# Padding between SBUF pools: six distances between weights and streamed rows in place of one

## The chip, the cores and the metric

One core of one Trainium2 chip. The metric is the device time of the whole program in microseconds (us). The kernel before was timed twice.

## The reference

The input `x` has 8 sequences of 3072 rows and 256 columns, all float32. The reference takes a real FFT along the 3072 rows of each sequence, mixes the 256 channels of the spectrum by two complex weight matrices, shrinks the result, transforms back, and puts every row through a gated feed-forward block of width 1536:

```python
X = np.fft.rfft(x, axis=1)
Yr = Xr @ w_r - Xi @ w_i + b_r
Yi = Xr @ w_i + Xi @ w_r + b_i
Y = soft(Yr) + 1j * soft(Yi)          # sign(v) * max(|v| - 0.01, 0)
y = np.fft.irfft(Y, n=3072, axis=1).reshape(-1, 256)
rms = np.sqrt(np.mean(y * y, axis=-1, keepdims=True) + 1e-06)
yn = y / rms * rms_g
out = (silu(yn @ w_gate) * (yn @ w_val)) @ w_out
```

## The kernel before, in words

**The products.** Most matrix products are made in float32r. A float32 operand is cut into a high part and the rest (two float32r tiles side by side), and a product is three matmuls: high by high, high by rest, rest by high. A matmul has a weight operand (`lhsT`, 128 x 128, loaded by a weight load of its own) and rows that stream beside it (`rhs`, 256 or 512 columns). The weight load of the next matmul runs beside the matmul that is streaming.

**The stages.** The FFT of 3072 is a 24-point part on VectorE (`first`, `dft8`, `dft3`) and twelve units of 128-point products on TensorE. In `unit` (L506) a unit is: forward (L530, bank `pf`, weights `as`, rows `F`, named `tab` in the profile), mixing (L570, L588, L592, bank `pm`, weights `xs` and, for the first unit, `d`; rows `wm`), and back (L633, L650, L655, bank `pb`, weights `G`, named `tab`; rows `ss`). The first sequence goes through `unit_start` (L672), whose mixing is at L710 with weights `xs` from pool `w2` and rows `wm`, and whose forward and back products (L688, L729) are plain float32. `transposes` (L862) turns four blocks of 128 rows at L867 with `ident`.

The feed-forward block runs in 576 steps: 48 tiles of 512 rows by 12 slices of 128 hidden columns. A step is `straight` (L892; six matmuls of 512 columns at L901 for the gate bank `g` and six for the value bank `v`) or `products` (L915; seven products of half the rows, three matmuls of 256 columns each, at L925), then `down` (L960), twelve matmuls of 256 columns into `acc`. The weights of the up products are `wb`, resident, and `tr` (called `tb` or `tr` in the profile), fetched for each step; the rows are `xn`. The weights of the down product are `hs`, the step's own result, and the rows are `wo`, fetched. 456 steps go by `products` and 120 by `straight`.

**What sets the order.** Every operation goes into a plan (`Plan`) with a due time and a cost; `schedule` plays the engines through and writes one fixed order for each engine. Forward, mixing and back products of the next sequence lie between the feed-forward steps of the one before. On TensorE runs of three matmuls of one kind alternate with runs of another. The plan knows nothing of addresses.

**Where tiles lie.** A pool is a stretch of SBUF, the same in each partition, and pools are laid one behind the other in the order in which they are made (L272 and L273): first `cp` (`wm`), `bp` (the sequences), `w1` (`F`, `ss` and others), `w2` (`xn`, `h`), `w4` (`wo`), which hold all streamed rows of the float32r products; then `wp`, which holds one tile of 320 bytes that nothing reads; then `cq` (`wb`), `q4` (`tr`), `q3` (`hs`), `q1` (`G`, `as`, `xs` and three tiles that are no weights), `q2` (empty) and `sp` (`ident`, biases and small things). All tiles of the pools before `sp`, but for the pad, are of a multiple of 512 bytes in each partition, and a weight operand is a slice of 512 bytes that begins at a multiple of 512 in its tile; rows begin at a multiple of 1024 in theirs. So each weight operand of the pools behind `wp` begins 320 bytes (modulo 512) from the rows beside it.

```python
wp.tile([P, 320], mybir.dt.uint8, name="shift")
```

The table `POOLS` (L326) says which tag lives in which pool with how many buffers.

Of the kernel before, what the change touches and what calls it, by code (L numbers as in the profile page):

```python
# [260 lines left out]
def fourier_glu_kernel(ctx: ExitStack, tc: tile.TileContext, x, w_r, w_i, b_r, b_i, wg, wv, wo, rg, tabs, units, tws, out):  # L261
# [3 lines left out]
    P = 128  # L265
# [3 lines left out]
    def sbuf(name, bufs):  # L269
        return ctx.enter_context(tc.tile_pool(name=name, bufs=bufs))  # L270

    cp, bp, w1, w2, w4 = sbuf("cp", 1), sbuf("bp", 2), sbuf("w1", 1), sbuf("w2", 2), sbuf("w4", 4)  # L272
    wp, cq, q4, q3, q1, q2, sp = sbuf("wp", 1), sbuf("cq", 1), sbuf("q4", 4), sbuf("q3", 3), sbuf("q1", 1), sbuf("q2", 2), sbuf("sp", 1)  # L273
    pu = ctx.enter_context(tc.tile_pool(name="pu", bufs=2, space=bass.MemoryType.PSUM))
    pv = ctx.enter_context(tc.tile_pool(name="pv", bufs=3, space=bass.MemoryType.PSUM))
    pa = ctx.enter_context(tc.tile_pool(name="pa", bufs=1, space=bass.MemoryType.PSUM))
# [3 lines left out]
    V, A, PE, G = nc.vector, nc.scalar, nc.tensor, nc.gpsimd  # L280

    wp.tile([P, 320], mybir.dt.uint8, name="shift")
    wm = cp.tile([P, 2, 2, 3, D], F32R, name="wm")
    wb = cq.tile([P, NF, 3, 2, P], F32R, name="wb")
    dw = [[dp.tile([P, 2, n], F32, name=f"d{c}{i}") for i in range(NF)] for c, n in (("t", 512), ("o", D), ("b", 512))]
# [33 lines left out]
    def add(n, f, r, w):  # L321
# [4 lines left out]
    POOLS = {  # L326
        "seq": (bp, 2), "F": (w1, 1), "t4": (w1, 1), "o": (w1, 1), "m": (w1, 1), "a": (w1, 1), "k": (w1, 1), "z": (w1, 1),
        "ss": (w1, 1), "xf": (w1, 1), "xn": (w2, 2), "h": (w2, 2), "wo": (w4, 4),
        "tr": (q4, 4), "hs": (q3, 3), "G": (q1, 1), "as": (q1, 1), "xs": (q1, 1), "t3": (q1, 1), "st": (q1, 1), "pq": (q1, 1),
        "gb": (pu, 2), "vb": (pv, 3), "acc": (pa, 1), "f": (pf, 1),  # L330
    }

# [949 lines left out]
```

## Time and profile before

| | us |
|---|---|
| median of two timed runs | 2841.64 (2840.09 to 2843.18) |
| the profiled execution's own time | 2839.71 |
| its span, from the first to the last instruction | 2838.0 |
| TensorE matmuls, busy (98% of the span) | 2787.4 |
| TensorE weight loads, busy (95%) | 2702.2 |
| VectorE, busy (81%) | 2297.4 |
| ScalarE, busy (67%) | 1906.8 |
| GpSimd, busy (3%) | 90.4 |

PE stands for TensorE's matmuls, PEld for its weight loads, DVE for VectorE, ACT for ScalarE, POOL for GpSimd. A line such as `L925 PE MATMUL v<-xn,tr` is the instructions of line 925 that write bank `v` from `xn` and `tr`. The time that a matmul is shown to take reaches past the start of the next one; the time from one start to the next is its pace. The timeline merges instructions of the same line and tiles that follow one another: its columns are the start of the first, the time to the end of the last, and, at the end of the line, how many they are. [...]

### The profile page before, as it was taken

The page shows a single profiled execution, that of the slowest core. Times are in us where ns is not written, and L with a number is a line of the kernel's source. Part 1 is how long each engine was busy: PE and PEld are TensorE (multiplying, and loading weights), DVE is VectorE, ACT ScalarE, POOL GpSimd, SP SyncE. Part 2 cuts the span into 40 slices and gives each one's busy share as a digit, 9 for nine tenths or more (in the row PEclk, how much of TensorE's full clock was granted, in tenths as well). Part 3 has the DMA queues.
Part 4 walks back from the last instruction along what each step waited for, and adds up shares of the span by engine and source line. Part 5 has one row for each costly group of instructions (what it writes and reads, how often), then busy time and mean ns, then how long its engine had stood idle before and what let it go on. Part 6 is the DMA issues. An engine that isn't in the chain of part 4 may idle for free.

```text
span 2838.0 us, 57978 instructions
## 1 busy us (share of the span) xinstructions
PE 2787.4 (98%) x22147; PEld 2702.2 (95%) x22147; DVE 2297.4 (81%) x4211; ACT 1906.8 (67%) x4518; POOL 90.4 (3%) x176
## 2 busy tenths in 40 slices
PE   7879999999999999999999999999999999999999
PEld 7768999999999999999999999999999999999999
DVE  9898779977897788977889778987779877866665
ACT  3464676777766777676776667767677677766665
POOL 0000000000000000000000000000000000000000
PEclk9989999999999999999999999999999999999999
DMA  6366665666656667566675666656665677646665
GB/s 213 129 217 201 203 218 174 216 217 216 214 179 214 216 216 231 165 211 212 212 233 172 210 214 220 215 184 210 213 224 190 192 224 220 198 132 223 208 218 171
DMA packets 247033, 577.77 MB, mean 204 GB/s; under 512 B 23393, under 2 KB 80098, under 8 KB 246754
## 3 DMA queue, kind: packets, MB, share of 16 engines
q1 hardware_dynamic: 222562, 485.97, 52.7%
q0 software_dynamic: 24192, 88.09, 10.7%
q8 instruction: 174, 2.85, 0.4%
q14 instruction: 105, 0.86, 0.1%
HBM read 534.65 MB, written 39.32 MB: 202 GB/s over the span
## 4 chain that ended last, share of the span: by engine, by line
PE 96%; DVE 3%; DMA 0%; ACT 0%; issue 0%; SPq 0%; ACTq 0%; DVEq 0%
PE acc L960 28%; PE v L925 22%; PE g L925 17%; PE v L901 6%; PE g L901 6%; PE pf L530 4%; PE pm L592 4%; PE pm L588 2%; PE pb L655 2%; PE pt L867 2%; PE pb L650 1%; PE pm L710 1%; PE pm L570 1%; PE pb L729 1%; PE pf L688 0%; PE pb L633 0%
## 5 line engine op out<-in xcount | busy, mean ns | idle before, releaser
L960 PE MATMUL acc<-wo,hs 128*128 128x256 f32 x6912 | 986.8, 279 | 11.0 <-ACT sq L751 9.0
L960 PEld LDWEIGHTS acc<-wo,hs 128*128 128x128 f32 x6912 | 888.9, 189 | 19.8 <-ACT sq L751 9.1
L925 PE MATMUL v<-xn,tr 128*128 128x256 f32 x4104 | 682.3, 280 | 0.5 <-ACT v L934 0.5
L925 PEld LDWEIGHTS v<-xn,tr 128*128 128x128 f32 x4104 | 567.6, 188 | 2.4 <-ACT v L934 0.7
L952 ACT ACTIVATE hs<-h 128x512 fp32r<-128x512 f32 x576 | 362.4, 629 | 209.9 <-PE acc L960 181.8
L953 DVE TENSOR_TENSOR hs<-h,hs 128x512 fp32r<-128x512 f32 x576 | 395.2, 686 | 83.3 <-ACT hs L952 83.2
L925 PE MATMUL g<-xn,wb 128*128 128x256 f32 x2736 | 457.9, 279 | 0.0
L938 DVE TENSOR_TENSOR y<-v,p 128x512 f32<-128x512 f32 x456 | 314.0, 689 | 174.1 <-PE v L925 165.8
L925 PEld LDWEIGHTS g<-xn,wb 128*128 128x128 f32 x2736 | 378.9, 188 | 0.0
L942 DVE TENSOR_TENSOR h<-h,y 128x512 f32<-128x512 f32 x456 | 313.5, 687 | 66.7 <-ACT h L941 63.6
L941 ACT ACTIVATE h<-v 128x256 f32<-128x256 f32 x456 | 174.0, 382 | 98.1 <-PE v L925 93.0
L925 PE MATMUL g<-xn,tr 128*128 128x256 f32 x1368 | 232.4, 279 | 0.0
L925 PE MATMUL v<-xn,wb 128*128 128x256 f32 x1368 | 232.3, 278 | 0.0
L934 ACT ACTIVATE v<-v 128x256 f32<-128x256 f32 x456 | 169.7, 372 | 92.7 <-PE v L925 90.5
L939 ACT ACTIVATE h<-g 128x256 f32<-128x256 f32 x456 | 174.4, 382 | 68.5 <-PE g L925 62.7
L931 ACT ACTIVATE v<-g 128x256 f32<-128x256 f32 x456 | 169.7, 372 | 73.2 <-PE g L925 69.6
L901 PE MATMUL g<-xn,wb 128*128 128x512 f32 x720 | 190.8, 400 | 1.2 <-DVE wb L810 0.5
L925 PEld LDWEIGHTS g<-xn,tr 128*128 128x128 f32 x1368 | 191.4, 188 | 0.0
L925 PEld LDWEIGHTS v<-xn,wb 128*128 128x128 f32 x1368 | 191.4, 188 | 0.0
L503 POOL DMA_DIRECT2D tab<-in_tabs_dram x168 | 89.6, 533 | 2358.8 <-PE pf L530 1434.3
L901 PEld LDWEIGHTS g<-xn,wb 128*128 128x128 f32 x720 | 129.9, 190 | 26.6 <-DVE wb L810 0.8
L530 PE MATMUL pf<-tab,as 128*128 128x256 f32 x1008 | 138.9, 278 | 0.0
(166 smaller groups left out, 4008.0 us busy)
## 6 DMA issues: line engine op xcount, KB each, us to landing
tr<-dt SPq DMA_DIRECT2D x456, 512.0 KB, 3.9
wo<-do SPq DMA_DIRECT2D x564, 256.0 KB, 3.3
tab<-in_tabs_dram POOLq DMA_DIRECT2D x168, 512.0 KB, 4.7
out_dram<-o SPq DMA_DIRECT2D x32, 512.0 KB, 3.6
seq<-in_x_dram SPq DMA_DIRECT2D x28, 512.0 KB, 5.4
tb<-db SPq DMA_DIRECT2D x27, 512.0 KB, 4.3
seq<-in_x_dram SPq DMA_DIRECT2D x25, 256.0 KB, 5.3
unit<-in_units_dram SPq DMA_DIRECT2D x12, 512.0 KB, 3.6
```

Source lines behind the costliest of these rows:

```text
L530: PE.matmul(ps[:, h, :], lhsT=r()[:, lp, ri, h * P:(h + 1) * P], rhs=f[:, rp, ri, :], start=(k + ri == 0), stop=(k == 2 and ri == 1),)
L901: PE.matmul((g, v)[k].flat(), lhsT=w(k, lp, c), rhs=xn()[:, rp, 2 * c:2 * c + 2, :].rearrange("p a b -> p (a b)"), start=((lp, rp, c) == t ...
L925: PE.matmul(dst(), lhsT=w(lp), rhs=xn()[:, rp, x, :], start=start and k == 0, stop=k == 2, skip_group_check=True)
L931: op("A", act(256), lambda _: A.activation(left(), p1(), AF.Copy), [one.tok], two.first)
L934: op("A", act(256), lambda _: A.activation(right(), left(), AF.Copy), [], [two.tok])
L938: op("V", dve(512), lambda _: V.tensor_tensor(y(), two(), p5().unsqueeze(1).to_broadcast([P, 2, 256]), ALU.add), [two.tok, p5.tok], y.first)
L939: op("A", act(256), lambda _: A.activation(s()[:, :256], p1(), AF.Silu), [one.tok], s.first)
L941: op("A", act(256), lambda _: A.activation(s()[:, 256:], right(), AF.Silu), [two.tok], [s.part("b")])
L942: op("V", dve(512), lambda _: V.tensor_tensor(s(), s(), y().rearrange("p a b -> p (a b)"), ALU.mult), [y.tok, s.part("b")], [s.tok])
L952: op("A", act(512), lambda _: A.activation(h()[:, 0], s(), AF.Copy), [s.tok], h.first)
L953: add(512, lambda f: f(h()[:, 1], s(), f32(h()[:, 0]), ALU.subtract), [s.tok], [h.tok])
L960: PE.matmul(o()[:, c, :], lhsT=h()[:, lp, c * P:(c + 1) * P], rhs=wo_()[:, rp, :], start=(i == 0 and k == 0 and c % 2 == 0), stop=(i == NF ...
```

## The change

The one pad of 320 bytes ahead of all weight pools is replaced by pads of 64 or 128 bytes ahead of single pools, so that the offsets add up. `q1` is split: `as`, `xs` and `G` get pools of their own (`qa`, `qx`, `qg`), and what was left of it stays in `q1`. The empty pool `q2` goes. The offsets, modulo 512, of what lies in each pool become: `cq` (`wb`) 64, `q4` (`tr`) 128, `q3` (`hs`) 192, `qa` (`as`, and `d`) 256, `qx` (`xs`) 384, `qg` (`G`) 448, and `q1` and `sp` 448 as well.

```diff
-    wp, cq, q4, q3, q1, q2, sp = sbuf("wp", 1), sbuf("cq", 1), sbuf("q4", 4), sbuf("q3", 3), sbuf("q1", 1), sbuf("q2", 2), sbuf("sp", 1)
+    homes = []
+    for name, bufs, shift in (("cq", 1, 64), ("q4", 4, 64), ("q3", 3, 64), ("qa", 1, 64), ("qx", 1, 128), ("qg", 1, 64), ("q1", 1, 0), ("sp", 1, 0)):
+        if shift:
+            homes.append((sbuf(f"wp{name}", 1), shift))
+        homes.append((sbuf(name, bufs), 0))
+    cq, q4, q3, qa, qx, qg, q1, sp = (p for p, shift in homes if not shift)
...
-    wp.tile([P, 320], mybir.dt.uint8, name="shift")
+    for k, (p, shift) in enumerate(homes):
+        if shift:
+            p.tile([P, shift], mybir.dt.uint8, name=f"shift{k}")
...
-        "tr": (q4, 4), "hs": (q3, 3), "G": (q1, 1), "as": (q1, 1), "xs": (q1, 1), "t3": (q1, 1), "st": (q1, 1), "pq": (q1, 1),
+        "tr": (q4, 4), "hs": (q3, 3), "G": (qg, 1), "as": (qa, 1), "xs": (qx, 1), "t3": (q1, 1), "st": (q1, 1), "pq": (q1, 1),
```

## Rows read from the trace of the kernel before

**Rows 1.** The page: busy time, granted clock in 40 slices, chain by engine.

```profile
PE 2787.4 (98%) x22147; PEld 2702.2 (95%) x22147; DVE 2297.4 (81%) x4211; ACT 1906.8 (67%) x4518; POOL 90.4 (3%) x176
...
PEclk9989999999999999999999999999999999999999
...
PE 96%; DVE 3%; DMA 0%; ACT 0%; issue 0%; SPq 0%; ACTq 0%; DVEq 0%
```

**Rows 2.** Stretch: length, busy (x) of PE, PEld, DVE, ACT, POOL, clock, DMA, GB/s.

```profile
250.00:2830.00 2580.00, 2578.76 (x20996) 2520.89 (x20995) 2066.52 (x3749) 1790.22 (x4276) 87.65 (x165) 1.00 0.65 206
```

**Rows 3.** Groups of TensorE, 250 to 2830 us: count, busy us, mean ns, idle.

```profile
L960 PE MATMUL acc<-wo,hs 128*128 128x256 f32 x6605 | 945.7, 279 | 0.8 <-DVE hs L953 0.8
L925 PE MATMUL v<-xn,tr 128*128 128x256 f32 x4104 | 682.3, 280 | 0.5 <-ACT v L934 0.5
L925 PE MATMUL g<-xn,wb 128*128 128x256 f32 x2736 | 457.9, 279 | 0.0
L925 PE MATMUL g<-xn,tr 128*128 128x256 f32 x1368 | 232.4, 279 | 0.0
L925 PE MATMUL v<-xn,wb 128*128 128x256 f32 x1368 | 232.3, 278 | 0.0
L901 PE MATMUL g<-xn,wb 128*128 128x512 f32 x564 | 146.9, 396 | 0.0
...
L901 PE MATMUL v<-xn,wb 128*128 128x512 f32 x282 | 96.5, 396 | 0.0
L901 PE MATMUL v<-xn,tb 128*128 128x512 f32 x282 | 96.4, 396 | 0.0
L655 PE MATMUL pb<-ss,tab 128*128 128x256 f32 x462 | 69.1, 279 | 0.0
...
L867 PE MATMUL pt<-ident,seq 128*128 128x128 f32 x360 | 54.0, 272 | 0.0
...
L650 PE MATMUL pb<-ss,tab 128*128 128x512 f32 x77 | 30.1, 392 | 0.0
L588 PE MATMUL pm<-wm,xs 128*128 128x512 f32 x77 | 30.1, 391 | 0.0
```

**Rows 4.** Timeline of TensorE: four transposes and what starts after them.

```profile
2627.83 0.60 PE L867 MATMUL pt<-ident,seq 128*128 128x128 f32 x4
2628.19 0.60 PE L925 MATMUL g<-xn,wb 128*128 128x256 f32 x3
```

**Rows 5.** Timeline of TensorE: twelve matmuls of 512 columns, first row and next step.

```profile
1510.45 1.56 PE L901 MATMUL g<-xn,wb 128*128 128x512 f32 x6
...
1513.25 1.53 PE L960 MATMUL acc<-wo,hs 128*128 128x256 f32 x12
```

**Rows 6.** Timeline of TensorE: 15 runs from the first row to the last.

```profile
1518.77 0.50 PE L925 MATMUL g<-xn,wb 128*128 128x256 f32 x3
...
1525.57 0.50 PE L925 MATMUL v<-xn,wb 128*128 128x256 f32 x3
```

**Rows 7.** Timeline of TensorE: 25 runs from the first row to the last.

```profile
1535.84 0.52 PE L925 MATMUL v<-xn,tr 128*128 128x256 f32 x3
...
1547.86 0.52 PE L960 MATMUL acc<-wo,hs 128*128 128x256 f32 x3
```

**Rows 8.** The first sequence's mixing: chain (start, length, pieces), then its weight loads.

```profile
39.77 5.75 PE pm L710 x48
...
L710 PEld LDWEIGHTS pm<-wm,xs 128*128 128x128 f32 x45 | 5.5, 192 | 0.0
```

**Rows 9.** Weight loads of the down product in the stretches of rows 6, 7.

```profile
L960 PEld LDWEIGHTS acc<-wo,hs 128*128 128x128 f32 x54 | 6.9, 188 | 0.0
...
L960 PEld LDWEIGHTS acc<-wo,hs 128*128 128x128 f32 x40 | 5.3, 189 | 0.0
```

**Rows 10.** Groups of VectorE, whole span: two operations on two SBUF tiles.

```profile
L953 DVE TENSOR_TENSOR hs<-h,hs 128x512 fp32r<-128x512 f32 x576 | 395.2, 686 | 83.3 <-ACT hs L952 83.2
...
L942 DVE TENSOR_TENSOR h<-h,y 128x512 f32<-128x512 f32 x456 | 313.5, 687 | 66.7 <-ACT h L941 63.6
```

## Prediction

> **What bounds the kernel now.** I read the page first. TensorE is busy 98% of the span and its weight loads 95%, the granted clock shows 9 tenths or more in all slices but the third, and 96% of the chain that ended last is PE [rows 1]. So the end is set by how many matmuls run and at what pace; no DMA and no other engine is late. Idle time of DVE and ACT costs nothing here.
>
> The duration of a matmul in the groups (279 ns) says little, since matmuls overlap. The pace from one start to the next is what counts. From 250 to 2830 us, at a clock of 1.00, 20,996 matmuls start in 2580 us [rows 2]. The groups of the same stretch [rows 3] tell what they are: 19,354 of 256 columns (the six rows of that form and seven smaller groups that are not shown, 996, 924, 385, 154, 126, 84 and 42), 1,282 of 512 columns (564 + 282 + 282 in the feed-forward, 77 + 77 in the spectrum), 360 transposes. Four transposes take 2627.83 to 2628.19, 90 ns each [rows 4], 32 us in all. Twelve of 512 columns take 1510.45 to 1513.25, 233.3 ns each [rows 5], 299 us in all. What is left, 2249 us over 19,354, is 116.2 ns for a matmul of 256 columns, the few waits included.
>
> That mean hides two paces. From 1518.77 to 1525.57, 15 runs with 60 matmuls of 256 columns go at 113.3 ns each [rows 6]. From 1535.84 to 1547.86, 25 runs with 102 of them go at 117.8 ns [rows 7]. Both stretches hold the same kinds (acc, g, v, with weights from `wb`, `tr` and `hs`), so within one distance the pace is a state of the stream: kept over a hundred matmuls, through changes of kind, until something disturbs it. If the mean is a mixture of the two, (117.8 - 116.2) / 4.5 = 36% of the matmuls go at the quick pace, a lower bound, since the waits are in the mean.
>
> The trace has one other distance for the same kind of matmul. In the first sequence's products (L710) the weights `xs` and the rows `wm` both lie in pools ahead of the pad: distance 0. There 48 matmuls take 5.75 us, 119.8 ns each, and one weight load takes 192 ns [rows 8], against 188 in the quick stretch and 189 in the slow one [rows 9]. So the distance matters, by 6.5 ns between 0 and the better state of 320.
>
> [...]
>
> **The change part by part.** Every tile that a weight load reads has a size divisible by 512 bytes, as have all slices taken of it, so the pad alone sets the distance. Before, all of them stand at 320. After: `wb` at 64, `tr` at 128, `hs` at 192, `as` (and d) at 256, `xs` at 384, `G` at 448. The unshifted tiles (`xn`, `wo`, `wm`, `F`, `ss`) stay. No instruction, wait, DMA or order is added, removed or moved; pool q2 held nothing. The split of q1 into four pools keeps one buffer for each tag.
>
> Counts by kind from [rows 3]: `hs` 6,605 at 192; `tr` 4,104 + 1,368 = 5,472 at 128, with 282 of 512 columns; `wb` 2,736 + 1,368 = 4,104 at 64, with 564 + 282 = 846; `as` 996 + 42 at 256; `xs` 1,435 at 384, with 77; `G` 462 + 154 + 84 = 700 at 448, with 77.
>
> The trace shows no pace for any of the six new distances, so each is bounded by the nearest rows: 113.3 ns below [rows 6], 119.8 above [rows 8]. I take 113.3 as a floor: neither of the two distances shows a stretch under it. Against the mean of 116.2 that is -2.9 to +3.6 ns for each. For 512 columns, twice these paces, 226.7 to 239.6, against 233.3.
>
> First term. 64 and 448 are one step of 64 either side of 0, where the pace is 119.8; half-way between that and today's mean is 118.0, and the nearest row is the slow pace, 117.8. I take that: (4,104 + 700) x 1.6 ns = 7.7 us, and (846 + 77) x 3.2 ns = 3.0 us. Bounds: -13.9 to +17.3 us for the 256-column ones, -6.1 to +5.8 for the others.
>
> Second term. 128, 192, 256 and 384 are two steps or more away from 0, and I leave their paces at today's mixture. But today a state survives a change of kind because all kinds have one distance. After the change, the distance jumps when the kind changes, which is every 4 matmuls (60 in 15 runs, [rows 6]). I let the first matmul after each jump pay the slow pace: (19,354 - 4,804) / 4 = 3,640, of which 36% are quick today: 1,310 x 4.5 ns = 5.9 us. Bounds: nothing, if the state survives; all 14,550 at the slow pace, 14,550 x 1.6 = 23 us.
>
> Edits at nothing. Transposes read `ident`, which moves from 320 to 448: 360 at 90 ns, and 1 ns on each would be 0.4 us. DVE's operands move too, but a DVE operation with operands at distance 320 (hs<-h,hs) takes 686 ns and one with both unshifted (h<-h,y) 687 [rows 10], so nothing is expected there; and DVE is not on the path. The first 250 us hold some 1,150 matmuls; the first sequence's products stay at distance 0, and the rest would change by some 2 us at most.
>
> Sum: 7.7 + 3.0 + 5.9 = 16.6 us. The profiled execution took 2839.71 us (span 2838.0), so 2856.3; the median of the two timed runs is 1.9 us above that execution, so 2858. If PE slows, nothing new becomes late: every other engine gains room.
>
> **The rivals.**
>
> Nothing changes (2840 to 2842): the distance matters at 0 alone, or the load's and the rows' phases at the moment of meeting are the same for all multiples of 64, or the pads are rounded away when pools are placed. For: two states live at one distance, so the state weighs as much as the distance. Against: [rows 6, 8] show that the 320 in the code does reach the chip. [...]
>
> The quick pace everywhere: six distances break whatever brings the slow state. Gain at most 2.9 x 19,354 = 56 us and 6.6 x 1,282 = 8.5 us, 65 us, so 2777 against the median; waits are within the 2.9 and don't go, so I put 2790. For: 113.3 holds for long stretches. Against: nothing in the change aims at the disturbances that end a quick stretch, and it adds jumps.
>
> Slower: 128 and 192, which carry 12,077 of the 19,354 matmuls, collide as 0 does. All six at 119.8: 3.6 x 19,354 = 70 us and 6.3 x 1,282 = 8 us, so 2920. With `hs` and `tr` alone it is 43 us, and with the first term 54 us: 2896. The point from which it is slower by over 2% (57 us) is a mean of 119 ns over all kinds. For: 119.8 was reached at the only other distance known, and a distance worse than 0 isn't excluded. Against: at 0 both reads begin in the same place, which no new distance does.
>
> **How the numbers follow.** Forecast 40%, nothing 23%, quick everywhere 12%, slower 25%. A measurement of this kernel tells about 2% from no change. Of the quick case half passes 2% (under 2785): 0.06. Of the slower case nearly all passes 2898, and a little of the forecast's tail: 0.27. The rest, 0.67, is within 2%. The range reaches down to 2795, short of the quick floor, and up to 2930, a little past all six at 119.8: some 1 in 10 is left out on either side.
>
> **What would show it.** With the distance right as the cause, the paces from start to start of `acc`, `g<-xn,wb`, `v<-xn,tr` part from each other in the profile after, where today they share one state; `wb` and `pb` (G) are at 117 ns or more. The weight load's mean goes with the pace (188 quick, 189 slow, 192 at 0). If the paces still come as long stretches of 113.3 and 117.8 that run through all kinds, the second term is wrong. If L710 in the first 100 us leaves 119.8, the distance isn't what set it. The forecast is wrong if any kind with over 4,000 matmuls stands outside 113 to 120 ns, or if PE's share of the chain falls below 96%.

## The result, and the profile after

| | us |
|---|---|
| before, median of two runs | 2841.64 |
| after, median of two runs | 2870.27 (2869.42 to 2871.11) |
| ratio | 1.0100, 95% interval 1.0075 to 1.0124 |
| the profiled execution before, after | 2839.71, 2871.11 |

The change costs 28.6 us, one per cent: slower, clear of the noise. The forecast was 2858, 16 us above before.

From the page after: busy time, granted clock, and the chain (the work that ended last, followed back from the end) by engine.

```profile
PE 2818.7 (98%) x22147; PEld 2735.0 (95%) x22147; DVE 2300.1 (80%) x4211; ACT 1909.0 (67%) x4518; POOL 90.0 (3%) x176
...
PEclk9989999999999999999999999999999999999999
...
PE 95%; DVE 3%; DMA 1%; issue 0%; ACT 0%; SPq 0%; ACTq 0%; DVEq 0%
```

The counts are those of [rows 1], the clock is the same, and PE is busy for 31.3 us more; DVE and ACT for 2 to 3 us. TensorE runs the same 22,147 matmuls in the same order, so all the lost time is pace. The stretch of [rows 2] after, with the same columns:

```profile
250.00:2830.00 2580.00, 2578.75 (x20730) 2521.87 (x20730) 2053.09 (x3724) 1774.41 (x4232) 87.27 (x165) 1.00 0.64 204
```

266 matmuls fewer start in the same 2580 us. In this stretch the groups of TensorE hold 360 transposes (32 us), 1,282 matmuls of 512 columns and 19,088 of 256. From the timeline, twelve matmuls of 512 columns and what follows them, to be held against [rows 5]:

```profile
1509.48 1.56 PE L908 MATMUL g<-xn,wb 128*128 128x512 f32 x6
...
1512.26 1.58 PE L967 MATMUL acc<-wo,hs 128*128 128x256 f32 x12
```

231.7 ns each against 233.3: the 512-column matmuls gain 2 us. What is left, 2251 us over 19,088, is 117.9 ns for a matmul of 256 columns against 116.2. 1.7 ns x 19,354 less those 2 us is 31 us, the difference of the two profiled executions (31.4).

The trace also tells which kinds lose. The table has the mean time from a matmul's start to the next start by the weights of the matmul (256 columns, 250 to 2790 us), and the difference times the counts of the prediction:

| weights | distance after | before, ns | after, ns | us |
|---|---|---|---|---|
| `tr` | 128 | 116.6 | 118.8 | 12.0 |
| `hs` | 192 | 115.9 | 117.3 | 9.3 |
| `as` | 256 | 115.4 | 119.4 | 4.2 |
| `wb` | 64 | 116.2 | 117.1 | 3.7 |
| `xs` | 384 | 116.3 | 118.5 | 3.1 |
| `G` | 448 | 116.9 | 117.0 | 0.1 |
| all with 512 columns | | | | -1.3 |

They add up to 31 us. The price of one kind shows in part on its neighbour: a matmul of `wb` with `tr` as the next weights takes 118.8 ns, 115.6 before. There the load of the next weights runs beside the last matmul of a run (in the trace after, loads of `wb` start at 1545.56 us, where the run of acc started at 1545.33 and that of `wb` starts at 1545.67).

How the pace looks now is seen in the timeline of TensorE, 1542.50 to 1546.72 us (first column start; the time to the next row's start, divided by the count, is the pace):

```profile
1542.50 0.52 PE L932 MATMUL g<-xn,wb 128*128 128x256 f32 x3
1542.86 0.51 PE L932 MATMUL g<-xn,tr 128*128 128x256 f32 x3
1543.21 0.87 PE L967 MATMUL acc<-wo,hs 128*128 128x256 f32 x6
1543.91 0.53 PE L932 MATMUL v<-xn,tr 128*128 128x256 f32 x3
1544.27 0.52 PE L967 MATMUL acc<-wo,hs 128*128 128x256 f32 x3
1544.63 0.52 PE L932 MATMUL v<-xn,tr 128*128 128x256 f32 x3
1544.98 0.50 PE L932 MATMUL g<-xn,wb 128*128 128x256 f32 x3
1545.33 0.50 PE L967 MATMUL acc<-wo,hs 128*128 128x256 f32 x3
1545.67 0.50 PE L932 MATMUL g<-xn,wb 128*128 128x256 f32 x3
1546.01 0.51 PE L932 MATMUL v<-xn,tr 128*128 128x256 f32 x3
1546.36 0.52 PE L932 MATMUL v<-xn,wb 128*128 128x256 f32 x3
1546.72 0.51 PE L932 MATMUL g<-xn,tr 128*128 128x256 f32 x3
```

36 matmuls take 4.22 us, 117.2 ns each, but not at one pace: a run of three takes 0.34 us (113.3 ns each: acc from 1545.33), 0.35 or 0.36 us (120 ns each: v<-xn,tr from 1543.91). The long stretches in which all kinds share one pace, [rows 6] and [rows 7], are gone here.

For the whole trace, let a succession be matmuls of one kind, one behind the other, and its pace the mean from start to start without its last matmul; it is quick up to 115 ns and slow from 117, and one with a time of 150 ns or more is left out. Then the longest stretch of quick successions has 33 matmuls after the change and 162 before.

The first sequence's mixing, whose distance the change leaves at 0, in the chain after (start, length, pieces), against [rows 8]:

```profile
39.52 5.75 PE pm L717 x48
```

It is the same to the hundredth of a microsecond.

### The profile page after: what moved, and what is told of

It is laid out like the page before. It is cut to its first block, busy times and chain, and to the rows that moved or that the text cites. A ratio compares the mean times of both kernels' runs of the same rounds, so it can differ in the third digit from the quotient of the medians.

```text
span 2869.3 us, 57978 instructions
## 1 busy us (share of the span) xinstructions
PE 2818.7 (98%) x22147; PEld 2735.0 (95%) x22147; DVE 2300.1 (80%) x4211; ACT 1909.0 (67%) x4518; POOL 90.0 (3%) x176
## 4 chain that ended last, share of the span: by engine, by line
PE 95%; DVE 3%; DMA 1%; issue 0%; ACT 0%; SPq 0%; ACTq 0%; DVEq 0%
PE acc L967 27%; PE v L932 22%; PE g L932 17%; PE g L908 5%; PE v L908 5%; PE pf L537 4%; PE pm L599 4%; PE pm L595 2%; PE pb L662 2%; PE pt L874 2%; PE pb L657 1%; PE pm L717 1%; PE pm L577 1%; PE pb L736 1%; PE pf L695 0%
## 5 line engine op out<-in xcount | busy, mean ns | idle before, releaser
L932 PE MATMUL v<-xn,tr 128*128 128x256 f32 x4104 | 691.8, 282 | 0.5 <-ACT v L941 0.5
```

The source lines that it names most:

```text
L932: PE.matmul(dst(), lhsT=w(lp), rhs=xn()[:, rp, x, :], start=start and k == 0, stop=k == 2, skip_group_check=True)
```

## The experiments

All run on one core of the same kind of chip, beside fresh runs of the kernel before (medians 2840.0 to 2841.1 us); a ratio is to these, with its 95% interval. In every kernel here only the weight operands move, and the rows stay where they are. So what is called a distance could as well be the place of the weight operand by itself, modulo some number of bytes: no run moves the rows, and the two are not told apart. The theories were:

- **A, jumps.** Any single distance lets the stream keep its states; what costs is that the distance changes with the kind.
- **B, a price for each distance.** Each distance has a pace of its own, and a kind brings that price with it.
- **C** (formed after the first four runs). As B, with the distance taken modulo 256.

### One distance for all: 128, 64, 192

The edit is the size of the one pad of the kernel before; for 128:

```diff
-    wp.tile([P, 320], mybir.dt.uint8, name="shift")
+    wp.tile([P, 128], mybir.dt.uint8, name="shift")
```

> The one pad of before, at 128 bytes in place of 320: every weight operand at distance 128, the distance that tr got in the change. Theory A (jumps: a uniform distance lets the stream keep a quick state, whatever the distance, and the loss of the change comes from the distance changing with the kind): the time is that of the kernel before within 0.5%, 2828 to 2856 us, and long stretches at 113.3 ns are back. Theory B (each distance has a pace of its own, and tr, whose runs stand at 117 to 120 ns after the change, has a bad one): 19,354 matmuls about 2 to 4 ns slower than the mean of 116.2 ns, 2880 to 2920 us.

2901.6 us, ratio 1.0217 (1.0202 to 1.0232).

> One pad of 64 bytes: every weight operand at distance 64, that of wb in the change. Theory A: within 0.5% of before, 2828 to 2856 us. Theory B: wb's pace after the change (about 117 ns) for all kinds, 2850 to 2865 us. If nearness to distance 0 is what costs: towards 119.8 ns, 2890 to 2920 us.

2839.9 us, ratio 1.0000 (0.9990 to 1.0009).

> One pad of 192 bytes: every weight operand at distance 192, that of hs in the change. Theory A: within 0.5% of before, 2828 to 2856 us. Theory B: hs's pace after the change (about 117.5 ns) for all kinds, 2855 to 2875 us.

2870.1 us, ratio 1.0108 (1.0092 to 1.0123).

The timelines of TensorE of the three, first 64, then 128, then 192, the first row of a stretch and the row that begins where it ends:

```profile
1519.91 0.50 PE L925 MATMUL g<-xn,wb 128*128 128x256 f32 x3
...
1525.01 0.84 PE L925 MATMUL v<-xn,tr 128*128 128x256 f32 x6
```

```profile
1548.97 0.52 PE L925 MATMUL g<-xn,wb 128*128 128x256 f32 x3
...
1561.07 1.11 PE L960 MATMUL acc<-wo,hs 128*128 128x256 f32 x8
```

```profile
1538.84 0.52 PE L960 MATMUL acc<-wo,hs 128*128 128x256 f32 x3
...
1559.33 0.52 PE L925 MATMUL v<-xn,tr 128*128 128x256 f32 x3
```

At 64, 45 matmuls in 5.10 us: 113.3 ns, the quick state of before. At 128, 102 in 12.10 us: 118.6 ns. At 192, 174 in 20.49 us: 117.8 ns, the slower pace of [rows 7]. Theory A falls in what it says of single distances: one can cost 61 us with no jump at all. Theory B stands for 128 and 192. Its figure for 64, 2850 to 2865 us from the pace of `wb` in the change, missed, and the price list is not what nearness to 0 would give: 64, the nearest to 0, is free.

### tr alone at 128

```diff
-    wp, cq, q4, q3, q1, q2, sp = sbuf("wp", 1), sbuf("cq", 1), sbuf("q4", 4), ...
+    wt, q4, wp, cq, q3, q1, q2, sp = sbuf("wt", 1), sbuf("q4", 4), sbuf("wp", 1), sbuf("cq", 1), ...
...
-    wp.tile([P, 320], mybir.dt.uint8, name="shift")
+    wt.tile([P, 128], mybir.dt.uint8, name="shift_t")
+    wp.tile([P, 192], mybir.dt.uint8, name="shift")
```

> Distance 128 for tr alone (its pool is moved ahead, behind a pad of 128 bytes), 320 for all the rest. Theory A: the distance jumps at nearly every second change of kind, so the quick state is lost about as often as in the change: most of the loss, 2855 to 2872 us, and acc and wb, whose own distance is unchanged, are slower too. Theory B: only matmuls beside a load of tr (5,472 and 282) are slower, by 2 to 4 ns: 2852 to 2865 us, with acc at its pace of before (mean 116.1 ns from start to start).

2859.3 us, ratio 1.0067 (1.0052 to 1.0082): 19.0 us slower. B's share is 61.3 us x 5,472 / 19,354 = 17.3 us; A had 15 to 32. The time alone doesn't tell them apart. A stretch of the timeline of TensorE shows who pays in it:

```profile
1541.07 0.87 PE L926 MATMUL v<-xn,tr 128*128 128x256 f32 x6
1541.77 0.51 PE L926 MATMUL g<-xn,wb 128*128 128x256 f32 x3
1542.11 0.50 PE L961 MATMUL acc<-wo,hs 128*128 128x256 f32 x3
1542.45 0.51 PE L926 MATMUL g<-xn,wb 128*128 128x256 f32 x3
1542.80 0.51 PE L926 MATMUL v<-xn,tr 128*128 128x256 f32 x3
1543.15 0.52 PE L926 MATMUL v<-xn,wb 128*128 128x256 f32 x3
1543.51 0.51 PE L926 MATMUL g<-xn,tr 128*128 128x256 f32 x3
```

Runs between `wb` and `hs`, which stand at 320, go at 0.34 us (1541.77 and 1542.11); `tr` takes 0.70 us for six (1541.07) and 0.35 for three (1542.80), and a run of `wb` that is followed by `tr` 0.35 or 0.36 (1542.45, 1543.15). So the price of `tr` shows on the neighbour too.

The whole trace shows that this is not all. A matmul of `wb` takes 119.8 ns where the next weights are `tr` (115.6 before), and one of `hs` 119.4 (115.7). But one of `wb` with `wb` next also goes from 115.5 to 116.9 ns. Of the loss 8 us lie on `tr`, 7 on `wb` and 5 on `hs`, and the longest stretch of quick successions has 45 matmuls. So the figure of B held and its account did not: it had `acc` at its pace of before. Here the quick state doesn't last through jumps between 320 and 128, as A had it.

### A jump without a bad distance; 384 and 256; 96

The jump is the split of the change with other pads: `wb`, `hs`, `xs` at 64, `tr`, `as`, `G` at 320.

```diff
-    for name, bufs, shift in (("cq", 1, 64), ("q4", 4, 64), ("q3", 3, 64), ("qa", 1, 64), ("qx", 1, 128), ("qg", 1, 64), ...
+    for name, bufs, shift in (("cq", 1, 64), ("q4", 4, 256), ("q3", 3, 256), ("qa", 1, 256), ("qx", 1, 256), ("qg", 1, 256), ...
```

> The split pools of the change with other pads: wb, hs and xs at distance 64, tr, as and G at 320. So the distance still jumps by 256 bytes at nearly every change of kind, but only between the two distances that, each alone, gave the time of before. Theory A (the jump itself costs): slower, 2850 to 2872 us, no long stretches of 113.3 ns. Theory C (the pace goes by the distance modulo 256, so 64 and 320 are one): 2834 to 2846 us, with the stretches of 113.3 and 117.8 ns at the same places as before.

2841.9 us, ratio 1.0002 (0.9993 to 1.0012). Its timeline of TensorE keeps one pace through 37 runs:

```profile
1518.49 0.50 PE L932 MATMUL g<-xn,wb 128*128 128x256 f32 x3
...
1534.13 0.50 PE L932 MATMUL g<-xn,tr 128*128 128x256 f32 x3
```

138 matmuls in 15.64 us, 113.3 ns, while the distance goes between 64 and 320 all the time. A jump of 256 bytes costs nothing here.

> One pad of 384 bytes. Theory C: the time and the pace of 128, 2895 to 2908 us, mean 119.0 ns from start to start. Against it, if the full 512 bytes count: the pace that xs showed in the change (118.4 ns), 2880 to 2892 us, or anything else.

2902.5 us in one run, beside 2901.6 for 128. Within runs of `tr` the traces of both show 119.0 ns.

> One pad of 256 bytes. Theory C: the pace of distance 0, 119.8 ns in the first sequence's mixing, for all kinds: 2841 us + 19,354 x 3.6 ns + 1,282 x 6.3 ns = 2919 us, 2905 to 2930. If the full 512 bytes count, as far from 0 as can be: 2840 to 2880 us.

2915.0 us in one run. The timeline of TensorE:

```profile
1560.03 0.88 PE L925 MATMUL v<-xn,tr 128*128 128x256 f32 x6
...
1569.38 0.52 PE L925 MATMUL g<-xn,wb 128*128 128x256 f32 x3
```

78 matmuls in 9.35 us: 119.9 ns, for all kinds, the pace that [rows 8] had at distance 0 for one kind in the first 100 us. Three pairs now agree modulo 256: 0 and 256, 64 and 320, 128 and 384. 192 and 448 were not compared.

> One pad of 96 bytes, half-way between 64 (time of before) and 128 (61 us slower). If the cost grows steadily from 64 to 128: 2860 to 2880 us. If what counts is which part of a line of 64 or 128 bytes the two reads share, an odd multiple of 32 is a class of its own: it could be the quick state alone, 113.3 ns throughout, 2775 to 2800 us, or as 128.

2885.8 us, ratio 1.0152 (1.0135 to 1.0169): above the steady case between 64 and 128, far from a quick class of its own, and not as 128 either.

### The rest of the circle: 32, 160, 224

> One pad of 32 bytes. 64 is at the time of before, 0 (by 256) 74 us above it. If the cost falls steadily from 0 to 64: 2870 to 2885 us. If only what lies near 64 is quick: 2900 to 2915 us. If 64 stands already on the far side of the best place: under 2836 us.

2890.0 us, ratio 1.0175 (1.0157 to 1.0194), between the first two cases.

> One pad of 160 bytes, half-way between 128 (61 us above before) and 192 (30 us above). If the cost goes steadily between steps of 64: 2880 to 2892 us. If odd multiples of 32 are dearer, as 96 was against 64: 2890 to 2910 us.

2921.5 us, ratio 1.0289 (1.0273 to 1.0305): above both cases, dearer than both its neighbours, the dearest of all.

> One pad of 224 bytes, half-way between 192 (30 us above before) and 256 (74 us above). Steady between the two: 2885 to 2900 us. With 0, 32, 64, 96, 128, 160 and 192 it completes the circle of 256 bytes in steps of 32; if none of them is under 2836 us, no single pad of such a step beats the one of before.

2863.4 us, ratio 1.0084 (1.0068 to 1.0100): below the range, cheaper than both its neighbours. So the price is no smooth curve. In us above before, around the circle of 256 bytes:

| distance | 0 | 32 | 64 | 96 | 128 | 160 | 192 | 224 |
|---|---|---|---|---|---|---|---|---|
| us | 74 | 50 | 0 | 45 | 61 | 81 | 30 | 23 |

(0 is the run at 256.) None of these pads beats the one of before.

### hs alone at 192

```diff
-    wp, cq, q4, q3, q1, q2, sp = sbuf("wp", 1), sbuf("cq", 1), sbuf("q4", 4), sbuf("q3", 3), ...
+    wh, q3, wp, cq, q4, q1, q2, sp = sbuf("wh", 1), sbuf("q3", 3), sbuf("wp", 1), sbuf("cq", 1), ...
...
-    wp.tile([P, 320], mybir.dt.uint8, name="shift")
+    wh.tile([P, 192], mybir.dt.uint8, name="shift_h")
+    wp.tile([P, 128], mybir.dt.uint8, name="shift")
```

> Distance 192 for hs alone (its pool is moved ahead, behind a pad of 192 bytes), 320 for all the rest. Theory B, that a kind brings the price of its own distance whatever its neighbours have: hs is 6,605 of the 19,354 matmuls, a third of what 192 for all cost (30 us): 10 us, 2846 to 2855 us. Theory A, that a jump costs by itself: more than that, 2855 to 2870 us. If the price is less where the distance changes every few matmuls, because no state of the bad distance has time to settle: under 2846 us.

2820.7 us, ratio 0.9934 (0.9916 to 0.9952): 19.3 us **faster** than before. Only the last case, open at its lower end, holds it, and no theory had foreseen a gain. Theory B, by which the prices of kinds add up, falls with it: it had +10 us. It is the quickest kernel of the study and beats both the kernel before and the changed one. Its timeline of TensorE, first where a slow stretch ends, then around a run that is held up:

```profile
1511.77 0.52 PE L926 MATMUL g<-xn,wb 128*128 128x256 f32 x3
1512.13 0.52 PE L926 MATMUL g<-xn,tr 128*128 128x256 f32 x3
1512.48 1.22 PE L961 MATMUL acc<-wo,hs 128*128 128x256 f32 x9
1513.54 0.50 PE L926 MATMUL v<-xn,tr 128*128 128x256 f32 x3
...
1527.48 0.50 PE L926 MATMUL g<-xn,tr 128*128 128x256 f32 x3
1527.82 0.55 PE L926 MATMUL v<-xn,tr 128*128 128x256 f32 x3
1528.21 0.87 PE L961 MATMUL acc<-wo,hs 128*128 128x256 f32 x6
1528.92 0.50 PE L926 MATMUL v<-xn,tr 128*128 128x256 f32 x3
1529.26 0.50 PE L926 MATMUL g<-xn,wb 128*128 128x256 f32 x3
1529.60 0.84 PE L961 MATMUL acc<-wo,hs 128*128 128x256 f32 x6
```

The stream is slow up to 1513.54 (the nine of acc take 1.06 us, 117.8 ns each) and quick right behind that run of `hs`: from 1513.54 to 1527.48, 123 matmuls at 113.3 ns, through 34 runs with `hs` at 192 among them. At 1527.82 a run is held up, the next run of acc is slow (six in 0.71 us), and behind it the stream is quick again. Before, the same run is held up in the same way, and behind it comes the slow stretch of [rows 7], 102 matmuls long:

```profile
1534.75 0.55 PE L925 MATMUL v<-xn,tr 128*128 128x256 f32 x3
1535.14 0.87 PE L960 MATMUL acc<-wo,hs 128*128 128x256 f32 x6
```

The whole trace bears this out. With `hs` alone at 192, 253 of the 265 successions of `hs` that go at the slow pace are followed by one at the quick pace, and 15 of 807 for the other kinds. Before, it is 1 of 462 for `hs`; with 192 for all it is 0 of 807 for `hs`. So neither the place in the program nor the distance of 192 by itself ends a slow stretch: it ends where the weights go from `hs` at 192 back to 320. The quick state mostly survives the same jump: 559 of 620 successions of `hs` at the quick pace are followed by one at the quick pace. The share of matmuls at 115 ns or less goes from 48% to 71%, and `hs` itself gains only 3 of the 19 us, the kinds that stayed at 320 the rest. Why the jump does this isn't known. The kernel also has the pool of `hs` moved ahead of the other weights, as the kernel with `tr` alone at 128 has that of `tr`; such a move without a new distance was not run.

## Why the prediction was right, and which of its steps were not

**What bounds the kernel** held: TensorE's pace alone, with no instruction moved and no other engine late.

**The distance matters, and both paces are real.** The profile after has matmuls at 113 and at 120 ns within 4 us, and the single distances outside the class of 64 and 320 cost 23 to 81 us. The rival "nothing changes" (2840 to 2842 us) fell: the change took 2870.3.

**The first term fell in its place.** It put the cost on `wb` at 64, "one step of 64 either side of 0", at the slow pace, 10.7 us with `G`. Distance 64 costs nothing at all: used for every kind it gives 2839.9 us against 2840.3. The nearest row (distance 0) pointed the wrong way, because the price is not a slope away from 0: 32 costs 50 us, 64 nothing and 96 again 45. In the change the term comes to 3 us in place of 10.7: 3.7 for `wb`, of which a good part lies in the matmuls beside a load of `tr` (118.8 ns, 115.6 before), 0.1 for `G`, and 0.9 gained at 512 columns.

**What the prediction left "at today's mixture" is what costs.** 128 used for all is 61 us dearer, 192 is 30, 256 is 74. By shares of 19,354 matmuls, `tr` (5,472 at 128) would bring 17 us, `hs` (6,605 at 192) 10, `xs` (1,435 at the price of 128, as 384 measured) 5, `as` (1,038 at 256) 4 and `G` (700 at 448, if that is as 192) 1: 37 us, against 28.6 measured. The table of the result has 28 us for `tr`, `hs`, `xs` and `as`, 512 columns included, where the prediction had 5.9. Where a kind runs by itself it has nearly the pace that its distance has for all: within runs of `as` 119.4 ns (119.9 with 256 for all), of `xs` 118.5 (118.7 with 384), of `tr` 118.3 (119.0 with 128).

**The second term was right in kind and wrong in sign at its place.** With the distances of the change the quick state does go: no stretch of quick successions longer than 33 matmuls is left after, where before one had 162. The mixture that the term starts from was 48% quick by the trace, where the prediction had 36% as a lower bound. But the term charged every jump with a slow matmul. Jumps between 64 and 320 cost nothing (2841.9 us, 2841.1 before), and with jumps of `hs` alone between 320 and 192 the kernel gains 19 us. The floor of 113.3 ns held as the pace of long stretches.

**So the sum was right by compensation.** +16.6 us was forecast and +28.6 measured; the missed price of `tr` is larger than what was wrongly charged to `wb`. That the two came out near each other is luck, and the range, 2795 to 2930 us, would have held an unchanged time too. `tr` alone at 128 gives +19.0 us and `hs` alone at 192 gives -19.3 us; with both and the smaller kinds the change gives +28.6, so prices of kinds don't add. With `hs` alone at 192, 253 of 265 successions of `hs` at the slow pace are followed by one at the quick pace; after the change it is only 78 of 659. A kernel with just `hs` and `tr` moved was not run, so which of the other distances takes the gain away stays open.

**Signs asked for.** The paces did part within 4 us of timeline, and the first sequence's mixing stayed at 5.75 us for 48. "`wb` and `pb` at 117 ns or more" came out by a hair (117.1 and 117.0) and says little, since `pb` stood at 116.9 before. The weight load's mean did not go with the pace: it is 188 ns after for `tr` as for `wb`, and 190 for `as`. The bound on PE's share of the chain (96%) was a bad sign: it is 95% after, with 1% of DMA in the chain, and the kernel with `hs` at 192, which is faster than before, has a lower share still (its page, chain by engine):

```profile
PE 94%; DVE 3%; DMA 1%; issue 0%; ACT 0%; SPq 0%; ACTq 0%; DVEq 0%
```

## What to carry to other kernels

When every matmul has a weight load of its own running beside it, the place of the weight operands is a knob worth trying: in this one kernel it goes from 81 us slower to 19 us faster (of 2840) with not one instruction changed. Scan it rather than interpolate: steps of 32 bytes over 256 went up and down here. Read the pace from start to start: the mean duration of the matmuls of acc is 279 ns before and after the change, while their pace goes from 115.9 to 117.3. The best of the uniform distances tried here (320 and 64, 2840 us) was not the best place for every kind (`hs` alone at 192: 2820.7 us): look for what ends a stretch at the slower pace, and try single kinds.

## What the runs showed of the hardware that was not expected

- The pace goes with the distance (or the place of the weights alone, with the rows unmoved) modulo 256 bytes as far as tried (0 and 256: 119.8 and 119.9 ns; 64 and 320: 2839.9 and 2840.3 us; 128 and 384: 2901.6 and 2902.5 us), not modulo the 512 bytes of a weight operand's row.
- The stream of float32r matmuls of 256 columns keeps one pace through long stretches: at 320 60 matmuls at 113.3 ns and 102 at 117.8, at 64 45 at 113.3, at 128 102 at 118.6, at 192 174 at 117.8, at 256 78 at 119.9. Before, a run held up at 1534.75 us is followed by the slow one, and the slow one lasts until four transposes start at 1548.22 us.
- One kind at a distance that is slow by itself (192 for all: +30 us) can make the whole quicker (192 for `hs` alone: -19.3 us): a slow succession of `hs` is followed by a quick one in 253 of 265 cases, in 1 of 462 before.
